# Seven block products in place of eight in one more quarter of two batches, and what moves with them

## The chip, the cores and the metric

The kernel runs on one core of a Trainium2 chip. The metric is the device time of one execution in microseconds (us), taken as the median of several runs. A profile shows one execution in detail; its times are counted from the first instruction.

## What is computed

Linear attention with cosine weights for 8 batches, 8 heads, 576 rows and 64 features, and behind it a channel mixer with a low-rank mixing over the sequence. Cut to what matters:

```python
r = np.maximum(x, 0.0)                                  # phi, of q and of k
phi = np.concatenate([r * c, r * s], axis=-1)           # cos and sin of the position
kv = np.einsum('bhsf,bhsd->bhfd', k_p, v)
x = num / den                                           # q_p @ kv over q_p @ sum(k_p)
h = xt @ U @ V                                          # rank 32, over the sequence
u = x + h.transpose(0, 2, 1)
out = u + np.maximum(u @ w_ch1, 0.0) @ w_ch2            # 512 -> 2048 -> 512
```

## The kernel before, in words

**Stages of a batch.** Each batch has 512 rows in the main part and 64 in a tail; the tails of two batches (a pair) are computed together. The attention of batch b gives x, then A (U against x), then u = x + VA. GpSimd, ScalarE and VectorE prepare q, k and v (`q_prep`, `k_prep` L305 and L307, `v_prep` L116). u in bfloat16 (`u_bf`, added by VectorE in `u_add`, L506) is transposed by DMAs that SP issues (`utr_dma`: L535 for the main part in two halves of features, L541 for the tail `uT_tl`). The first product (`hid = relu(u @ w_ch1)`) gives hid in 16 blocks j of 128 x 512. The second product reads hid and gives the output.

**Strassen in the first product.** A plain block (`g1_main`, L710) is 4 matmuls of 512 columns, and ScalarE's relu (L717). Four blocks (a quarter, m) can instead be taken as a 2 x 2 block product with 7 parts (`g1_part`, L653) of 4 matmuls of 256 columns: sums of weights `sa` (made once by VectorE, L591), differences of u^T `tb` (VectorE, `uT_form`, L608, four per batch), partial results that ScalarE copies out of PSUM (`pw`, L114), additions by VectorE (L678), and a relu of what was added. In batches 4 and 6 that relu is on ScalarE (L670), two slots later; elsewhere on VectorE (L675). One part is finished by ScalarE alone (L687). `HALF` (L1046) is the order of such a half of the first product: eight slots, in which the 7 parts take turns with 4 plain blocks. `MIXED` (L815) says which halves of which batch are done so: both in 3 and 5, the first alone in 4 and 6, and all 16 blocks of batch 7 by `LAST`. `FULL` is the list of batches with both.

**Strassen in the second product.** For batches 1 to 7 it is done in 7 parts of two halves (`W_SEQ`, L860: 1 1 2 6 6 2 7 5 5 7 3 3 4 4; `w_part`, L874, matmuls L892). Its left sides are S1 to S4, made of hid by VectorE (`hid_form`, L841, operations L857) in two halves of rows each. S3 is written over a block of hid; part 7 reads it, part 3 reads S4, part 6 S2, part 5 S1. The result is put together in `o_sb`: ScalarE copies parts 1, 6 and 5 out of PSUM (L114), VectorE adds parts 2, 7, 3 and 4 (L912), GpSimd adds u (`add_u`, L912 on POOL), and a DMA writes it out (L755, issued by GpSimd for batches below 6, else by SP).

**The order.** It is written out by hand: `slots` is a list of small units of TensorE work, `starts[b]` the number of batch b's first slot, here called G. A first product has 16 slots; an odd batch has 4 more for the tails of its pair (`g1_tail`, L741, which read `uT_tl`); a second product has 14. `put` hangs other work on a slot: it is issued behind that slot's matmuls. Each engine, SP's queue included, works strictly in the order in which its instructions were issued. `attention_plan` (L1129) hangs the attention of batch b on the slots of batches b - 2 and b - 1. For b = 5 and 7, G being the start of batch b - 1, the five `x_unit`s stand on slots G + 5, 8, 10, 12, 14 where batch b - 1 is in `MIXED`, and on G + 5, 8, 11, 13, 15 where it is in `FULL`; A, u and the transposes follow two slots and more after the last. `d0` (L1188) says which half of u is added and transposed first.

The two lines that decide where u's tail goes in these batches:

```python
late_t = 3 if b == 5 and b - 1 in FULL else 0 if b - 1 in FULL else 1 if b - 1 in MIXED else 0
put(*((u_at + 1, u_tail, *T1) if b < 4 else (u_at + 3 + d0 + late_t, u_tail, *X1S)))
put(u_at + 4 + d0 + late_t, utr_dma, 4, 5)
```

SP also carries the transposes of q (`qtr_dma`, L413 and L408) and the loads of q, k and v for the batch after (`loads`, L93, L80, L87). In the plan of batch 6 they stand on G + 23 and 24 (q's transposes) and G + 24 (the loads of q for batch 7), G being the start of batch 4.

Of the kernel before, what the change touches and what calls it, by code (L numbers as in the profile page):

```python
# [17 lines left out]
def kernel(  # L18
# [13 lines left out]
    B = 8  # L32
# [79 lines left out]
    def cast(eng, o, i):  # L112
        if eng is nc.scalar:
            nc.scalar.activation(out=o, in_=i, func=AF.Copy, bias=0.0, scale=1.0)  # L114
        else:
            eng.tensor_copy(out=o, in_=i)  # L116
# [150 lines left out]
    def bank(shape, dt, tag, bufs, name):  # L267
        if tag == "x":
            return ps.tile([P, 2, 512], FP32, tag="X", bufs=1, name=name)[:, 0, 0 : shape[1]]
        if tag in ("oA", "oB"):  # L270
            return ps_rest[1].tile(shape, dt, tag=tag, bufs=bufs, name=name)
        if tag == "O":
            t = ps_rest[2].tile([P, 2, 512], FP32, tag=tag, bufs=bufs, name=name)
            return t if len(shape) == 3 else t[:, 0, 0 : shape[1]]
        return ps.tile(shape, dt, tag=tag, bufs=bufs, name=name)
# [317 lines left out]
    def uT_block(b, dh, r):  # L593
        return uT[b][:, 2 * dh : 2 * dh + 2, 2 * r : 2 * r + 2, :].rearrange(
            "p d c t -> p d (c t)"
        )

    def uT_form(b, n):
        if b not in tb:
            tb[b] = pool.tile([P, 4, 2, 256], BF16, tag="tb", bufs=1, name="tb")  # L600
        t = tb[b]
        a, b_ = (
            (uT_block(b, 0, 1), uT_block(b, 0, 0)),
            (uT_block(b, 1, 1), t[:, 0]),
            (uT_block(b, 1, 1), uT_block(b, 0, 1)),
            (uT_block(b, 1, 0), t[:, 1]),
        )[n]
        V_.tensor_tensor(out=t[:, n], in0=a, in1=b_, op=ALU.subtract)  # L608
# [156 lines left out]
    def o_alloc(b, r):  # L765
        if (b, r) not in o_sb:
            o_sb[b, r] = pool.tile([P, 2, DM], FP32, tag="o_sb", bufs=2, name="o_sb")
        return o_sb[b, r]
# [43 lines left out]
                in_=o_s[i * TS : i * TS + TS, :],  # L812
            )

    MIXED = {3: (0, 2), 4: (0,), 5: (0, 2), 6: (0,)}  # L815
    FULL = [b for b, ms in MIXED.items() if 2 in ms]
    HD = DM // 2
    KB = NJ // 2
# [3 lines left out]
    def w2_block(i, h, r=slice(0, KB)):  # L822
        return w2_h[:, r, i, h * HD : h * HD + HD]
# [13 lines left out]
    def hid_block(b, i, r, rows=slice(0, KB)):  # L837
        h = hid[b].rearrange("p (k i) t -> p k i t", i=2)
        return h[:, rows, i, r * 256 : r * 256 + 256]

    def hid_form(b, n, half):  # L841
        if (b, n) not in s_forms:
            s_forms[b, n] = (
                hid_block(b, 0, 1) if n == 3 else
                pool.tile([P, KB, 256], BF16, tag=f"S{n}", bufs=1, name=f"S{n}")
            )
        r = slice(half * 4, half * 4 + 4)
        o = s_forms[b, n][:, r, :]
        if n == 1:
            a, b_, op = hid_block(b, 0, 1, r), hid_block(b, 1, 1, r), ALU.add  # L850
        elif n == 2:
            a, b_, op = s_forms[b, 1][:, r, :], hid_block(b, 0, 0, r), ALU.subtract
        elif n == 3:
            a, b_, op = hid_block(b, 0, 0, r), hid_block(b, 0, 1, r), ALU.subtract
        else:
            a, b_, op = hid_block(b, 1, 0, r), s_forms[b, 2][:, r, :], ALU.subtract
        V_.tensor_tensor(out=o, in0=a, in1=b_, op=op)  # L857
# [7 lines left out]
    def store_w(b, c, r):  # L865
        if b == 1:
            later.append(lambda: store(store_eng(b), b, c, o_sb[b, r]))
        else:
            store(store_eng(b), b, c, o_sb[b, r])
# [4 lines left out]
    def w_part(b, n):  # L874
        p, half = W_SEQ[n]
        lhs, rhs, to = {
            1: (lambda: hid_block(b, 0, 0), w2_block(0, 0), 0),
            2: (lambda: hid_block(b, 1, 0), w2_block(1, 0), 1),
            3: (lambda: s_forms[b, 4], w2_block(1, 1), 0),
            4: (lambda: hid_block(b, 1, 1), T[3], 2),  # L880
            5: (lambda: s_forms[b, 1], T[0], 0),
            6: (lambda: s_forms[b, 2], T[1], 0),
            7: (lambda: s_forms[b, 3], T[2], 2),
        }[p]
        lhs = lhs()
        opens = p in (1, 2, 7)
        if opens and half == 0:
            w_ps[to] = bank([P, DM], FP32, *(G3 if to else T1), f"w_ps{to}")
        res = w_ps[to].rearrange("p (g n) -> p g n", g=2)
        for k_ in range(half * 4, half * 4 + 4):  # L890
            for g in range(2):
                nc.tensor.matmul(  # L892
                    out=res[:, g, :], lhsT=lhs[:, k_, g * P : g * P + P], rhs=rhs[:, k_, :],
                    start=(opens and k_ == 0 and g == 0),
                    stop=(k_ == KB - 1 and g == 1), skip_group_check=not opens,
                )
        for f in ({0: (4,), 2: (3,)} if b == B - 1 else {0: (1, 2), 1: (4,), 2: (3,)}).get(n, ()):
            hid_form(b, f, 1)
        if half == 0:
            return  # L900

        def by_d(t):
            return t.rearrange("p c (d n) -> p d c n", n=P)

        def u(r, h):
            return u_bf[b][:, 2 * h : 2 * h + 2, 2 * r : 2 * r + 2, :]

        def o(r, h):
            return o_alloc(b, r)[:, :, h * HD : h * HD + HD]

        def add(eng, o_, x, y):
            eng.tensor_tensor(out=o_, in0=x, in1=y, op=ALU.add)  # L912

        def add_u(r, h):
            add(G_, by_d(o(r, h)), by_d(o(r, h)), u(r, h))

        if p == 1:
            cast(A_, o(0, 0), res)
            add_u(0, 0)
        elif p == 6:  # L920
            cast(A_, o(1, 0), res)
            add_u(1, 0)
        elif p == 5:
            cast(A_, o(1, 1), res)
        elif p == 2:
            add(V_, o(0, 0), o(0, 0), res)
        elif p == 7:
            add(V_, o(1, 1), o(1, 1), res)
            add_u(1, 1)
        elif p == 3:  # L930
            add(V_, by_d(o(0, 1)), u(0, 1), by_d(res))
            store_w(b, 0, 0)
        else:
            add(V_, o(1, 0), o(1, 0), res)
            store_w(b, 2, 1)
# [104 lines left out]
    slots, second, starts = [], [], {}  # L1040

    def lay(units, in_second):
        slots.extend(units)
        second.extend([in_second] * len(units))
# [3 lines left out]
    def first_units(b):  # L1048
        starts[b] = len(slots)

        def unit(names, m):
            def go():
                for n in names:
                    if n[0] == "s":
                        g1_main(b, 4 * m + int(n[1]))
                    else:
                        g1_part(b, m, int(n))

            return go

        for m in (0, 2):
            if m in MIXED.get(b, ()):
                lay([unit(n.split(), m) for n in HALF], False)
            else:
                lay([lambda j=j: g1_main(b, j) for j in range(4 * m, 4 * m + 8)], False)
        for i in range(4 * (0 < b)):
            n = 12 + 2 * i if b == 1 else (9, 11, 17, 18)[i] if b in MIXED else 8 + i
            beside.setdefault(starts[b] + n, []).append(
# [28 lines left out]
    def second_units(b):  # L1097
        lay([lambda n=n: w_part(b, n) for n in range(14)], True)
# [30 lines left out]
    def attention_plan(b):  # L1129
# [3 lines left out]
        def put(at, f, *a):  # L1133
            plan.append((at, lambda: f(b, *a)))
# [17 lines left out]
        else:  # L1152
# [19 lines left out]
            elif b - 1 in FULL:  # L1172
                kv_at, x_at = G + 1, [G + i for i in ODDX]
            elif b - 1 in MIXED:
                kv_at, x_at = G + 1, [G + i for i in X5]
# [17 lines left out]
        if odd:  # L1193
            late_t = 3 if b == 5 and b - 1 in FULL else 0 if b - 1 in FULL else 1 if b - 1 in MIXED else 0
            put(*((u_at + 1, u_tail, *T1) if b < 4 else (u_at + 3 + d0 + late_t, u_tail, *X1S)))
# [237 lines left out]
    def put(at, thunk):  # L1433
        todo.setdefault(at, []).append(thunk)

    put(15, lambda: gate(w2_bf[0:1, 4, 0:1]))
    s6 = starts[B - 2]
    for n in range(4):
        for m in (0, 2):
            put(starts[2] + (-4, -3, -1, 1)[n], lambda n=n, m=m: w1_form(n, m))  # L1440
            put(s6 - 6 + n, lambda n=n, m=m: w1_form(n, m + 1))
        for b in MIXED:
            put(starts[b] - 4 + n, lambda b=b, n=n: uT_form(b, n))
        put(s6 + 24 + n, lambda n=n: uT_form(B - 1, n))
        put(starts[B - 1] + len(LAST) + 5 + 2 * n, lambda n=n: tl_form(n))
    put(starts[3] - 2, split_o)
    put(70, release)
# [41 lines left out]
```

## Time and profile before

| | us |
|---|---|
| median of 3 runs | 291.23 (291.1 to 293.08) |
| the profiled execution | 291.12 |
| its span, first to last instruction | 289.3 |
| TensorE (PE) busy | 284.5 |
| VectorE (DVE) busy | 217.1 |
| ScalarE (ACT) busy | 173.3 |
| GpSimd (POOL) busy | 75.6 |
| first product of batch 4, first matmul | 160.13 |
| second product of batch 4 | 176.05 to 189.68 |
| first matmul of the tails of batches 4 and 5 | 204.7 |
| second product of batch 6 | 238.01 to 251.62 |

What lies between the span and the execution's own time is 1.8 us. Matmuls are pipelined: a row gives 379 ns for one of 512 columns, but the next starts after about 216 ns, so the spacing is read from long rows of the chain, not from the mean of one.

### The profile page before, as it was taken

To read this page: it belongs to the slowest core of one execution; us is meant where nothing else is said; L and a number is where in the kernel's file an instruction comes from. 1 tells how busy PE (TensorE), PEld (TensorE's weight loads), DVE (VectorE), ACT (ScalarE), POOL (GpSimd) and SP (SyncE) were. 2 spreads that over 40 slices of the span, in tenths; PEclk is the share of its full clock that TensorE was granted. 3 is DMA by queue.
4 is the path that set the end of the run, shared out by engine and by line. 5 is a ranking of instruction groups with operands and counts; after the bars stand their busy time and mean duration, and the time that the engine had idled before them with its cause. 6 is when DMAs were issued, how large, how long until landed. Compare 5 with 4: busy or idle time off the path is not lost.

```text
span 289.3 us, 7481 instructions
## 1 busy us (share of the span) xinstructions
PE 284.5 (98%) x3086; PEld 208.5 (72%) x3086; DVE 217.1 (75%) x440; ACT 173.3 (60%) x302; POOL 75.6 (26%) x111
## 2 busy tenths in 40 slices
PE   8999999999999999999999999999999999999995
PEld 6876455545987546876987656876888657999884
DVE  4879738886898777548896278848899579669954
ACT  2965651576587466986686577786795762167110
POOL 8330600050026301851043502341034003100320
PEclk9999999999999999999999999999999999999999
DMA  6999999999989999899929994589974301320023
GB/s 203 336 284 252 290 208 275 258 171 157 291 206 145 190 372 210 163 312 223 302 59 183 290 289 122 77 222 204 242 144 107 122 1 39 86 116 2 0 87 133
DMA packets 85447, 53.32 MB, mean 184 GB/s; under 512 B 53990, under 2 KB 83078, under 8 KB 85414
## 3 DMA queue, kind: packets, MB, share of 16 engines
q1 hardware_dynamic: 78998, 41.62, 63.1%
q0 software_dynamic: 6272, 11.17, 15.7%
q8 instruction: 24, 0.39, 0.6%
q14 instruction: 9, 0.07, 0.1%
q10 hardware_dynamic: 144, 0.07, 0.1%
HBM read 36.86 MB, written 9.44 MB: 160 GB/s over the span
## 4 chain that ended last, share of the span: by engine, by line
PE 98%; DVE 1%; issue 0%; DVEq 0%
PE w_ps L892 30%; PE g_ps L710 26%; PE al_ps L653 6%; PE gt_ps L741 5%; PE o_ps L781 5%; PE be_ps L653 5%; PE w_ps L202 3%; PE x_ps L439 3%; PE kv_ps L364 3%; PE ot_ps L801 2%; PE ot_ps L994 2%; PE a_ps L465 1%; PE va_ps L495 1%; PE t_ps L382 1%; PE t_ps L394 1%; PE g_ps L727 0%
## 5 line engine op out<-in xcount | busy, mean ns | idle before, releaser
L710 PE MATMUL g_ps<-uT,w_bf 128*128 128x512 bf16 x346 | 84.2, 379 | 0.0
L717 ACT ACTIVATE hid<-g_ps 128x512 bf16<-128x512 f32 x88 | 52.2, 597 | 35.8 <-PE g_ps L710 30.6
L912 POOL TENSOR_TENSOR o_sb<-o_sb,u_bf 128x512 f32<-128x512 f32 x21 | 29.8, 1419 | 123.8 <-ACT o_sb L114 106.2
L710 PEld LDWEIGHTS <-w_bf 128*128 128x128 bf16 x346 | 31.8, 98 | 29.1
L892 PEld LDWEIGHTS <-hid 128*128 128x128 bf16 x448 | 43.0, 98 | 6.3
L892 PEld LDWEIGHTS <-S 128*128 128x128 bf16 x336 | 32.5, 98 | 4.2
L678 DVE TENSOR_TENSOR hid<-pw,be_ps 128x512 bf16<-128x512 f32 x30 | 20.6, 686 | 19.4 <-ACT pw L114 11.1
L892 PE MATMUL w_ps<-w_bf,hid 128*128 128x256 bf16 x224 | 27.9, 273 | 0.0
L892 PE MATMUL w_ps<-T,hid 128*128 128x256 bf16 x224 | 27.9, 273 | 0.0
L114 ACT ACTIVATE pw<-al_ps 128x512 f32<-128x512 f32 x30 | 17.8, 596 | 15.6 <-PE al_ps L653 7.9
L892 PE MATMUL w_ps<-T,S 128*128 128x256 bf16 x224 | 26.9, 273 | 0.0
L114 ACT ACTIVATE o_sb<-w_ps 128x512 f32<-128x512 f32 x21 | 12.5, 597 | 19.7 <-PE w_ps L892 16.2
L912 DVE TENSOR_TENSOR o_sb<-o_sb,w_ps 128x512 f32<-128x512 f32 x21 | 14.3, 682 | 11.7 <-ACT o_sb L114 5.5
L506 DVE TENSOR_TENSOR u_bf<-x_bf,va_ps 128x1024 bf16<-128x1024 bf16 (+1 forms) x20 | 19.6, 998 | 3.4 <-PE va_ps L495 2.6
L449 DVE TENSOR_TENSOR x_bf<-x_ps,rec 128x512 bf16<-128x512 f32 x28 | 19.4, 692 | 1.0
L305 ACT ACTIVATE k_p<-kst,sinw 128x512 bf16<-128x512 f32 x26 | 17.8, 713 | 0.0
L116 POOL CAST v_ext<-vst 128x512 bf16<-128x512 f32 x24 | 15.8, 698 | 6.9 <-issue 3.2
L653 PEld LDWEIGHTS <-sa 128*128 128x128 bf16 x160 | 14.8, 98 | 3.3 <-issue 0.2
L741 PE MATMUL gt_ps<-uT_tl,w_bf 128*128 128x128 bf16 x256 | 16.4, 219 | 0.0
L781 PE MATMUL o_ps<-w_bf,hid 128*128 128x512 bf16 x64 | 15.6, 379 | 0.0
L755 POOL DMA_DIRECT2D out_dram<-o_sb x12 | 7.6, 631 | 30.3 <-DVE o_sb L789 22.8
L741 PEld LDWEIGHTS <-w_bf 128*128 128x128 bf16 x256 | 15.0, 98 | 0.4
(191 smaller groups left out, 495.0 us busy)
## 6 DMA issues: line engine op xcount, KB each, us to landing
qst<-in_q_dram SPq DMA_DIRECT2D x14, 512.0 KB, 5.9
kst<-in_k_dram SPq DMA_DIRECT2D x14, 512.0 KB, 7.8
vst<-in_v_dram SPq DMA_DIRECT2D x12, 512.0 KB, 8.3
out_dram<-o_sb POOLq DMA_DIRECT2D x12, 512.0 KB, 5.0
w_bf<-in_moe_w_ch_dram POOLq DMA_DIRECT2D x8, 512.0 KB, 10.3
out_dram<-o_sb SPq DMA_DIRECT2D x4, 512.0 KB, 3.7
qst<-in_q_dram SPq DMA_DIRECT2D x2, 640.0 KB, 5.8
kst<-in_k_dram SPq DMA_DIRECT2D x2, 640.0 KB, 13.8
```

What stands on the lines that cost most here:

```text
L114: nc.scalar.activation(out=o, in_=i, func=AF.Copy, bias=0.0, scale=1.0)
L305: nc.scalar.activation(out=o, in_=i, func=AF.Relu, bias=0.0, scale=w)
L449: nc.vector.tensor_tensor(out=x_of(b, c, rows).rearrange("p (g i d) -> p g i d", g=2, d=D), in0=view[:, :, :, 0:D], in1=rec[rows].unsqueez ...
L506: nc.vector.tensor_tensor(out=u_bf[b][:, d0 : d0 + n], in0=x_bf[b].rearrange("p c (d n) -> p d c n", n=P)[:, d0 : d0 + n], in1=t.rearrange ...
L653: nc.tensor.matmul(out=res[:, k_, :], lhsT=lhs[:, d, k_, :], rhs=rhs[:, d, :], start=(opens and k_ == 0 and d == 0), stop=(k_ == 1 and d = ...
L678: V_.tensor_tensor(out=o, in0=x, in1=res, op=ALU.add)
L710: nc.tensor.matmul(out=g_ps.rearrange("p (c t) -> p c t", c=4), lhsT=w1_bf[:, d, j * P : j * P + P], rhs=uT[b][:, d, :, :], start=(d == 0) ...
L717: nc.scalar.activation(out=hid[b][:, j, :], in_=g_ps, func=AF.Relu, bias=0.0, scale=1.0)
L741: nc.tensor.matmul(out=g_ps[:, jj, :], lhsT=w1_bf[:, d, j * P : j * P + P], rhs=uT_tl[pr][:, d, :], start=(d == 0), stop=(d == 3),)
L781: nc.tensor.matmul(out=o, lhsT=hid[0][:, j, cc * P : cc * P + P], rhs=w2_bf[:, j, :], start=(j == 0), stop=(j == NJ - 1),)
L892: nc.tensor.matmul(out=res[:, g, :], lhsT=lhs[:, k_, g * P : g * P + P], rhs=rhs[:, k_, :], start=(opens and k_ == 0 and g == 0), stop=(k_ ...
L912: eng.tensor_tensor(out=o_, in0=x, in1=y, op=ALU.add)
```

## The change

Four edits:

- `MIXED` has both halves for batches 4 and 6 too: 4 blocks in each go from plain to 7 parts. Since `FULL` is made of `MIXED`, batches 4 and 6 are in it now, and the plans of batches 5 and 7 take the other branch: x on G + 5, 8, 11, 13, 15; u and its transposes a slot later; the second half of u's features first (`d0` = 2); u's tail and its transpose on G + 26 and G + 27 for batch 5 (before: G + 21 and G + 22), and on G + 23 and G + 24 for batch 7.
- In the second product of batches 1 to 6 the second half of S3 is made one slot ahead of that of S4, where S4 was ahead.
- GpSimd's additions of u for parts 1 and 6 are issued behind VectorE's addition of part 2, both together.
- The differences of u^T come later: slots -3, -2, 0 and 2 from the batch's start (before: -4 to -1); for batch 7 slots -2, -1, 0 and 2 (before: -6 to -3).

```diff
-    MIXED = {3: (0, 2), 4: (0,), 5: (0, 2), 6: (0,)}
+    MIXED = {3: (0, 2), 4: (0, 2), 5: (0, 2), 6: (0, 2)}
...
-        for f in ({0: (4,), 2: (3,)} if b == B - 1 else {0: (1, 2), 1: (4,), 2: (3,)}).get(n, ()):
+        for f in ({0: (4,), 2: (3,)} if b == B - 1 else {0: (1, 2), 1: (3,), 2: (4,)}).get(n, ()):
             hid_form(b, f, 1)
...
         if p == 1:
             cast(A_, o(0, 0), res)
-            add_u(0, 0)
         elif p == 6:
             cast(A_, o(1, 0), res)
-            add_u(1, 0)
...
         elif p == 2:
             add(V_, o(0, 0), o(0, 0), res)
+            add_u(0, 0)
+            add_u(1, 0)
...
         for b in MIXED:
-            put(starts[b] - 4 + n, lambda b=b, n=n: uT_form(b, n))
-        put(s6 + 24 + n, lambda n=n: uT_form(B - 1, n))
+            put(starts[b] + (-3, -2, 0, 2)[n], lambda b=b, n=n: uT_form(b, n))
+        put(starts[B - 1] + (-2, -1, 0, 2)[n], lambda n=n: uT_form(B - 1, n))
```

## The prediction

> **What bounds the kernel now.** I read the page first (busy times and chain), then TensorE's waits and the chain in order of time, then the timelines of VectorE, SP and GpSimd around batch 4, where the change is.
>
> ```profile
> span 289.3 us, 7481 instructions
> PE 284.5 (98%) x3086; PEld 208.5 (72%) x3086; DVE 217.1 (75%) x440; ACT 173.3 (60%) x302; POOL 75.6 (26%) x111
> ...
> PE 98%; DVE 1%; issue 0%; DVEq 0%
> ```
>
> TensorE is busy for 98% of the span and makes 98% of the chain. A busy PE can still be stretched, so the list of TensorE's waits is needed; it has one line, at the start of the program:
>
> ```profile
> PE w_ps L202 <- DVE zero L125: 1.2, 1, 1.2
> ```
>
> In the chain in order of time (start, length, what) stalls shorter than a listed wait show as pieces that take longer than their like:
>
> ```profile
> 112.33 12.25 PE w_ps L892 x112
> ...
> 171.38 1.73 PE g_ps L710 x8
> ...
> 189.84 0.44 PE al_ps L653 x4
> ...
> 204.88 0.89 PE gt_ps L741 x16
> ...
> 222.14 0.54 PE al_ps L653 x4
> ```
>
> From these: a 512-column matmul costs 1.73 / 8 = 0.216 us of TensorE, a 256-column one 12.25 / 112 = 0.109. Four parts' matmuls take 0.44; at 222.14 they take 0.54, so batch 6 starts 0.1 late. From about 60 us on I find no other stall above 0.05. So removed TensorE work shortens the run one for one, and anything late for TensorE lengthens it.
>
> VectorE, the busiest helper, in batches 4 and 5; SP's queue; a GpSimd addition:
>
> ```profile
> 177.60 0.69 DVE L857 TENSOR_TENSOR S<-S,hid 128x1024 bf16<-128x1024 bf16 x1
> ...
> 181.34 1.28 DVE L857 TENSOR_TENSOR hid<-hid 128x1024 bf16<-128x1024 bf16 x2
> ...
> 212.23 1.54 DVE L857 TENSOR_TENSOR S<-hid,S 128x1024 bf16<-128x1024 bf16 x1
> ```
>
> ```profile
> 181.05 5.61 SPq L535 DMA_TRANSPOSE uT<-u_bf  x2
> 186.75 1.22 SPq L541 DMA_TRANSPOSE uT_tl<-u_tl  x1
> 188.07 1.21 SPq L413 DMA_TRANSPOSE q_tlT<-q_tl  x1
> 189.39 8.26 SPq L408 DMA_TRANSPOSE q_pT<-q_p  x2
> 197.70 0.62 SPq L93 DMA_DIRECT2D qst<-in_q_dram  x1
> 198.37 0.63 SPq L80 DMA_DIRECT2D qst<-in_q_dram  x1
> 199.04 1.34 SPq L87 DMA_DIRECT2D qst<-in_q_dram  x1
> ```
>
> ```profile
> 211.89 1.33 POOL L912 TENSOR_TENSOR o_sb<-o_sb,u_bf 128x512 f32<-128x512 f32 x1 [15.48 <-ACT o_sb L114]
> ```
>
> The S3 pair ends at 182.62, and part 7 of the second product, which reads it, starts at 182.68: no slack. SP needs 8.26 us for q's two transposes. And the S4 operation at 212.23 takes 1.54 us where its like takes 0.69, because it began while a GpSimd addition was running.
>
> **Part 1, the matmuls.** A quarter goes from 16 x 0.216 = 3.46 us to 28 x 0.109 = 3.06: 0.40 less, 0.79 in the two batches. Beside it, in each quarter: VectorE gets 3 additions of 0.69; ScalarE reads PSUM 8 times as before and gets 3 relus of 0.62. From 168 to 176 ScalarE was busy 5.2 us; 1.9 more fit. VectorE was busy 5.7; with 2.1 more it is full, so it has to be followed (part 2).
>
> The row against a rule: the Trainium skill, TensorE: Matmul & The Clock Gate, section Back-to-back issue gap, gives sustained spacings of 81 ns for 128 columns and 131 for 512, set by weight load and matmul together. A straight line gives an estimate of 98 for 256, and by it the quarter goes from 2.10 to 2.74 and the change costs 1.3 us. The trace disagrees: 216 and 109 in long rows. By the rows the change saves 0.79.
>
> **Part 2, x later, and S3 ahead of S4.** Batch 5's last x comes a slot later, behind VectorE's addition of part 4: PE is done with that part at about 175.4, the addition and the x (0.17, 0.20, 0.69) run to 177.4, where the trace has 176.51. A's matmuls read it at about 177.8: covered by 0.4. From the start of that last 0.69 at 176.7 the steps between starts, from the rows of 175 to 183, are 0.61, 0.72, 0.62, 0.39, 0.60, 0.60, 0.39, 0.60 (S1, S2, a q_prep, S3, S4, a q_prep, S4, S3) and the last takes 0.68: S3 is whole at 181.9. TensorE would now be at part 7 at 182.68 - 0.40 - 0.45 = 181.83, the 0.45 being u's tail matmuls and their gap (182.32 to 182.68 and 0.09), which come later now. A stall of 0.1; bounds 0 and 0.5. In batch 6 no q_prep stands between, so 0. ScalarE's relu of part 4, for which VectorE's second half of S4 waits, ends near 177.0, before S4 is due at 180.5. Were it late, S3 and both u_adds would queue behind it; the edit sets one S3 half free of that.
>
> **Part 3, GpSimd's additions.** Where they stood, VectorE no longer loses time: at 212.23 it gains 0.85, at 146.60 0.9. That ends no TensorE wait by itself: 0. Both additions now follow part 2's. In batch 5 that is at about 216.4. A k_prep that begins at 216.7 is held to about 218.1; the weight sums behind it run through while GpSimd waits (as at 219.84, where an addition took 2.61), then the second addition holds one of the next sums for about 0.6. VectorE's addition of part 3 ends near 222.15 (222.03 before), and batch 6's first matmuls wait for its bank: 0.1 more. Bounds: -0.1 (the old stall gone) and 1.4 (the second addition goes at once, and part 4 stalls 0.4 and batch 6 one more us). Part 4's addition and the stores, which wait for GpSimd, have over 1 us; at the end of the program the sums for the tails (L954) have 4 us.
>
> **Part 4, u and u^T.** The half of u^T that the first matmuls of batches 5 and 7 read is now the second transpose. Batch 5: VectorE's u_adds follow S3; the last starts at 183.4 and ends at 184.6; landing takes 3.0 to 3.7 us here, so 187.7 to 188.4, needed at 189.3: covered by 0.9. Batch 7 has about 2 us. Bounds: 0, and 2.9 by the slowest row (7.5 us at 110.53, behind loads of v). The later differences of u^T (0.42 each) are due two slots after the batch's start at the earliest; VectorE has a gap there: 0. Issue order on VectorE makes the addition of part 4 wait behind the first two; it has 1 us.
>
> **Part 5, u's tail.** Its transpose was issued at 186.75, landed 2.4 us later, and is read at 204.7: 15 us of cover. Now SP reaches it behind q's three transposes and three loads of q. SP: the second u^T at 184.65 takes 1.2 to 2.4 (181.05's pair shows both), so q_tlT goes at 186.0 to 187.2, by 0.9 to 2.1 earlier than 188.07, and so does the rest: the last load of q at 196.9 to 198.1 instead of 199.04. That load landed 7.0 us after its issue; now 203.9 to 205.1. A transpose issued directly behind a load landed 0.5 us after it (q_tlT at 120.67), so the tail of u^T lands at 204.4 to 205.6, middle 205.0. TensorE wants it at 204.7 less 0.3 (0.40 saved, 0.1 lost): 204.4. Stall 0.6. Bounds: 0, if it doesn't queue behind the loads (2.4 after its issue), and 3.2, if it lands 2.5 behind the load, as u^T at 110.53 did behind v. A stall here also hides part 3's 0.1. The loads of k behind it come 1.3 us of issue later, with over 8 us until they are read.
>
> **Sum.** -0.79 + 0.1 (S3) + 0.6 (tail) = -0.1 on the profiled execution's 291.12 (span 289.3 and 1.8 around it): 291.0. The median of the runs, 291.23, stands 0.1 above that execution; I leave that inside the range.
>
> **Rivals.**
> - *The tail is in time.* SP takes the short issue times and the queue empties sooner: -0.79 + 0.1 + 0.1 = 290.5. For it: 7 us of landing includes loads of k that were served in between. 25%.
> - *The tail is later still, and the kernel slower.* The DMA engines are full from 191 on; landing 2.5 behind the load gives a stall of 1.6 to 3.2. It decides from 0.7 us of stall (landing after 205.1) on; middle 292.2, up to 293.6. For it: the row at 110.53. Against: that one stood behind three loads of v that had themselves waited. 15%.
> - *GpSimd holds VectorE.* Two additions back to back keep the path that both use; part 3's upper bound, 291.12 - 0.7 + 1.4 = 291.8. The Trainium skill, SBUF — State Buffer, section Who interferes with whom, says that whoever issues first has it for the whole instruction. By that rule GpSimd's second addition could win. The 2.61 us at 219.84 show it losing. 5%.
> - *The half of u^T is late*: 7.5 us, twice: about 295. Against: no load is ahead of it. 3%.
> - *The 256-column matmuls don't keep their pace*, as at 222.14 (0.54 for four): 28 x 0.135 = 3.8, 0.3 more per quarter instead of 0.4 less: 291.8. The 1104 such matmuls of the trace speak against it. 1%. The rule of part 1 would lead to this side too.
>
> **How the numbers follow.** The forecast (a stall of 0.2 to 1.2 at the tails, 290.6 to 291.6) has 45%, the rivals as said, and 6% are left for a wait that I have not seen. The range 290.2 to 292.6 takes in the forecast, the tail in time, GpSimd and most of the later tail: 8 in 10. 1% of 291 is 2.9 us, about what a measurement of this kernel can tell from no change. Faster by that needs four times the saved work: 2%. Slower by it needs the late half of u^T or something unseen: 5%. Within 1%: 93%.
>
> **What would show it.** g_ps rows at L710 fall by 32 matmuls and L653 gains 56. In the chain: a piece of the tails (L741) near 204.4 with a gap ahead of it, or a wait of TensorE for the transpose of uT_tl, which SP issues near 198; if there is none, part 5 is wrong. A short gap before part 7 near 181.9 shows part 2; the 0.54 at batch 6's start shows part 3. A time outside 290.2 to 292.6 would mean a wait of TensorE that I have not named.

## The result, and the profile after

| | before | after |
|---|---|---|
| median of 20 runs each, us | 291.1 (290.73 to 293.08) | 294.18 (291.58 to 295.86) |
| ratio of the runs, 95% interval | | 1.008 [1.0055, 1.0104] |
| the profiled execution, us | 291.12 | 291.69 |
| its span, us | 289.3 | 289.9 |

The forecast was 291.0 (290.2 to 292.6) and no change within 1%. By the ratio of the runs the kernel became slower by 0.8%: clear of the noise, but inside that 1% (the two medians alone differ by 1.06%). Its median lies 1.6 us above the range. The profiled execution of after lies near the shortest of its own runs. Two more executions, profiled later beside a before of 291.61, took 296.31 and 296.83, more than any of the 20. In two of the 20 runs of after (295.05 and 295.86) the mean granted clock of TensorE is 0.994 and 0.993, in the others 0.998 or more. So there are two questions: what costs 0.6 in the profiled execution where 0.1 less was forecast, and what makes the runs of the same kernel differ by 4 us.

The page of after, against the lines shown for before. PE still has 98% of the span, but no longer 98% of the chain: VectorE (DVE) has 4% of it and a DMA 3%. The DMA is a load of v at the program's start (5.75 to 15.44 us), and almost half of VectorE's share lies at the start too. What bears on the change is the rest of VectorE's share, between 215.8 and 223.0.

```profile
span 289.9 us, 7553 instructions
PE 283.1 (98%) x3110; PEld 209.3 (72%) x3110; DVE 220.5 (76%) x446; ACT 175.5 (61%) x308; POOL 71.6 (25%) x111
...
PE 90%; DVE 4%; DMA 3%; SPq 0%; issue 0%; DVEq 0%
```

TensorE's waits in the same execution (total, times, longest). Before had only the one for `zero`. Of the new ones two lie in the first 45 us (0.4 and 0.2 us); the other two are both for VectorE's additions at L912:

```profile
PE al_ps L653 <- DVE o_sb L912: 1.0, 1, 1.0
...
PE w_ps L892 <- DVE o_sb L912: 0.3, 1, 0.3
```

They lie at the end of batch 5's second product. By the distances between matmuls TensorE loses 0.47 us ahead of part 4 (which starts at 220.14) and 1.16 ahead of batch 6's first matmul (at 223.04), where before lost 0.11. The timeline of VectorE there (start, length, what; x2 is a pair):

```profile
215.68 1.78 DVE L307 TENSOR_SCALAR k_p<-kst,cosw 128x512 bf16<-128x512 f32 x2
217.38 1.71 DVE L591 TENSOR_TENSOR sa<-w_bf 128x512 bf16<-128x512 bf16 x2
...
219.41 0.68 DVE L912 TENSOR_TENSOR o_sb<-o_sb,w_ps 128x512 f32<-128x512 f32 x1
220.00 1.71 DVE L591 TENSOR_TENSOR sa<-sa,w_bf 128x512 bf16<-128x512 bf16 x2
...
222.31 0.67 DVE L912 TENSOR_TENSOR o_sb<-u_bf,w_ps 128x512 f32<-128x512 bf16 x1
```

and of GpSimd:

```profile
215.84 2.62 POOL L912 TENSOR_TENSOR o_sb<-o_sb,u_bf 128x512 f32<-128x512 f32 x2 [20.00 <-DVE o_sb L912]
...
220.16 1.27 POOL L912 TENSOR_TENSOR o_sb<-o_sb,u_bf 128x512 f32<-128x512 f32 x1 [1.70 <-DVE o_sb L912]
```

The reader is to see three pairs of 1.7 to 1.8 us, each of which overlaps one of GpSimd's three additions, and that the additions of parts 7 (219.41) and 3 (222.31), for which TensorE waits, stand behind them. A pair of L591 that GpSimd leaves alone takes 0.74 (below).

SP's queue of after, around the transpose of u's tail:

```profile
187.32 6.33 SPq L408 DMA_TRANSPOSE q_pT<-q_p  x2
...
196.40 0.63 SPq L87 DMA_DIRECT2D qst<-in_q_dram  x1
197.13 2.00 SPq L541 DMA_TRANSPOSE uT_tl<-u_tl  x1
```

It is issued at 197.13 and lands 7.0 us later, at 204.09. TensorE starts the tail's matmuls at 204.15, right behind those before them: nothing is lost in this execution, and nothing is spare.

### The profile page after: what moved, and what is told of

It reads as the page before. It is cut to its first block, busy times and chain, and to the rows that moved or that the text cites. A ratio compares the mean times of both kernels' runs of the same rounds, so it can differ in the third digit from the quotient of the medians.

```text
span 289.9 us, 7553 instructions
## 1 busy us (share of the span) xinstructions
PE 283.1 (98%) x3110; PEld 209.3 (72%) x3110; DVE 220.5 (76%) x446; ACT 175.5 (61%) x308; POOL 71.6 (25%) x111
## 4 chain that ended last, share of the span: by engine, by line
PE 90%; DVE 4%; DMA 3%; SPq 0%; issue 0%; DVEq 0%
PE w_ps L892 28%; PE g_ps L710 24%; PE al_ps L653 7%; PE be_ps L653 5%; PE gt_ps L741 5%; PE o_ps L781 5%; DMA vst<-in_v_dram 3%; PE x_ps L439 3%; PE kv_ps L364 3%; PE ot_ps L801 2%; PE ot_ps L994 2%; DVE sa L591 1%; PE a_ps L465 1%; PE va_ps L495 1%; PE t_ps L382 1%; DVE k_p L307 1%
## 5 line engine op out<-in xcount | busy, mean ns | idle before, releaser
L710 PE MATMUL g_ps<-uT,w_bf 128*128 128x512 bf16 x314 | 77.0, 379 | 0.0
L717 ACT ACTIVATE hid<-g_ps 128x512 bf16<-128x512 f32 x80 | 47.4, 597 | 31.8 <-PE g_ps L710 26.6
L912 POOL TENSOR_TENSOR o_sb<-o_sb,u_bf 128x512 f32<-128x512 f32 x21 | 26.4, 1272 | 111.8 <-DVE o_sb L912 111.8
L710 PEld LDWEIGHTS <-w_bf 128*128 128x128 bf16 x314 | 29.1, 98 | 25.9
L678 DVE TENSOR_TENSOR hid<-pw,be_ps 128x512 bf16<-128x512 f32 x36 | 24.7, 686 | 18.3 <-PE be_ps L653 9.7
L114 ACT ACTIVATE pw<-al_ps 128x512 f32<-128x512 f32 x36 | 21.3, 595 | 18.1 <-PE al_ps L653 8.9
L912 DVE TENSOR_TENSOR o_sb<-o_sb,w_ps 128x512 f32<-128x512 f32 x21 | 14.3, 683 | 12.0 <-ACT o_sb L114 7.2
L653 PEld LDWEIGHTS <-sa 128*128 128x128 bf16 x192 | 17.7, 98 | 4.0 <-issue 0.2
L653 PEld LDWEIGHTS <-w_bf 128*128 128x128 bf16 x144 | 14.0, 98 | 4.7 <-issue 1.2
L741 PE MATMUL gt_ps<-uT_tl,w_bf 128*128 128x128 bf16 x256 | 16.4, 219 | 0.0
```

What stands on the lines that cost most here:

```text
L653: nc.tensor.matmul(out=res[:, k_, :], lhsT=lhs[:, d, k_, :], rhs=rhs[:, d, :], start=(opens and k_ == 0 and d == 0), stop=(k_ == 1 and d = ...
L678: V_.tensor_tensor(out=o, in0=x, in1=res, op=ALU.add)
L710: nc.tensor.matmul(out=g_ps.rearrange("p (c t) -> p c t", c=4), lhsT=w1_bf[:, d, j * P : j * P + P], rhs=uT[b][:, d, :, :], start=(d == 0) ...
L717: nc.scalar.activation(out=hid[b][:, j, :], in_=g_ps, func=AF.Relu, bias=0.0, scale=1.0)
L741: nc.tensor.matmul(out=g_ps[:, jj, :], lhsT=w1_bf[:, d, j * P : j * P + P], rhs=uT_tl[pr][:, d, :], start=(d == 0), stop=(d == 3),)
```

## The experiments

Two theories, and a rival. **T1**: GpSimd's two additions, back to back, hold VectorE at the end of batch 5's second product and cost 1.4 us in every run. **T2**: the tail's transpose, now behind q's transposes and loads on SP, lands late by an amount that differs from run to run; that is the spread and the higher median. **R**: something else, such as the new order of u^T's halves. Medians below are of 6 to 12 runs each, beside runs of before on the same chip.

**e1: the tail early.** 

```diff
-late_t = 3 if b == 5 and b - 1 in FULL else 0 ...
+late_t = 0 if b == 5 and b - 1 in FULL else 0 ...
```

> After with one number changed: the transpose of u's tail for batch 6 is issued on SP ahead of q's transposes and the loads of q, as far up as before. T2 (the tail's landing sets the median and the spread of after): the median comes down by about 2.5 us to 291.7, with the runs within about 1 us, and the profile keeps TensorE's waits of 0.47 and 1.05 us at the end of batch 5. T1 (the two additions on GpSimd are the whole of the loss): it stays at 294.2 with the spread of after. Rival R (the new order of u^T's halves or other transfers): 294.2 as well, with another wait at a batch's start in the slow runs.

Measured: 292.77 (292.5 to 294.77), before 291.32. The spread is gone (11 of 12 runs within 0.6 us), as T2 says, and the waits of 0.47 and 1.16 us stay. The median misses 291.7 by 1.1: u's tail, three slots earlier, makes TensorE wait about 0.9 us in batch 4 for VectorE's `u_bf` (ahead of L518). The late slot of the tail's matmuls has its reason; only the place of the transpose on SP has not.

**e2: the additions back.** `add_u(0, 0)` and `add_u(1, 0)` again behind the copies of parts 1 and 6, in all batches.

> After with GpSimd's two additions of u back behind parts 1 and 6, as before the change. T1: TensorE's waits of 0.47 and 1.05 us at parts 4 of batch 5 and 3 of batch 6 go (to under 0.2 us in sum), the profiled execution is about 1.4 us shorter than after's 291.69. If T2 alone makes the spread, the median is some 1.4 us under after's (292.8) and the spread stays as wide; if T1 makes the spread too, the median is 290.5 and the runs lie within 1 us.

Measured: 294.12 (291.82 to 297.67), before 291.32. Four of the 12 runs took 296.4 to 297.7, with a mean granted clock of 0.994 or less; the other eight have a median of 292.5. T1's two waits go, but as much comes elsewhere: 0.97 us ahead of part 7 of batch 4, and 0.24 and 0.5 in batch 6. The spread stays. Two of TensorE's waits in its profiled execution (294.46):

```profile
PE gt_ps L741 <- DMA uT_tl<-u_tl: 1.8, 1, 1.8
...
PE w_ps L892 <- DVE hid L857: 0.8, 1, 0.8
```

The first is T2 caught in the act; the second shows that the additions were moved for a reason. VectorE's S3 has no slack, and what stands ahead of it is held: beside GpSimd's addition at 178.89 a `q_prep` takes 1.38 us (at 179.13) where its like in after takes 0.47 (at 178.33), and all that VectorE has queued behind it, S3 too, comes 0.9 us later.

**e3: both undone.** e1's and e2's edits together.

> Both of these in one kernel: tail early and additions behind parts 1 and 6; what is left of the change is Strassen's algorithm in batches 4 and 6, S3 ahead of S4, and u^T's halves in the other order. T1 and T2 together: 290.3 to 290.6 in nearly all runs, about 0.6 us under the kernel before. Rival R: 292.5 to 294 with the spread kept.

Measured: 293.33 (292.59 to 295.05), before 291.32. That is 2.7 to 3.0 us over what T1 and T2 gave, and inside the time that the rival R gave. But its profile shows no wait for the tail's transpose. It collects the costs of both undoings (0.97 in batch 4 and 0.24 and 0.5 in batch 6 as in e2, 0.9 in batch 4 as in e1), and 0.4 twice around batch 5 that neither of them has. Undoing an edit everywhere is not the same as taking away its harm.

**e4: only the loads of q behind the tail.**

```diff
-at_load = (F + 8, ...
+at_load = (F + (12 if b == 6 else 8), ...
```

> After with the three loads of q for batch 7 issued four slots later, so that on SP the tail's transpose stands behind q's two transposes but ahead of those loads. If the loads are what holds the tail: its landing comes 3 us or more ahead of batch 6's need and the median is 291.7, as with the tail early. If q's transposes alone hold it: median and spread stay at 294.2. T1's waits of 0.47 and 1.05 us stay in both.

Measured: 292.17 (291.56 to 293.46), before 291.32. The tail lands at 200.3 where TensorE wants it at 204.6; the spread is half as wide and the median is 2.0 us under after's. T1's waits stay (0.48 and 1.16). Behind q's transposes alone the tail still takes 6.2 us from issue to landing (2.4 in before), but that leaves 4 us to spare. So it is the loads that take it past the time of its need.

**e9: both cures.** e4's edit, and the additions back at parts 1 and 6 in batch 5 alone.

```diff
         if p == 1:
             cast(A_, o(0, 0), res)
+            if b == 5:
+                add_u(0, 0)
...
         elif p == 2:
             add(V_, o(0, 0), o(0, 0), res)
-            add_u(0, 0)
-            add_u(1, 0)
+            if b != 5:
+                add_u(0, 0)
+                add_u(1, 0)
```

> The loads of q for batch 7 behind the tail's transpose (as in e4), and GpSimd's two additions of u behind parts 1 and 6 in batch 5 alone; in batches 4 and 6 they stay behind part 2. T1 (the two back to back additions cost 1.4 us in batch 5, and only there) with T2: the waits of 0.48 and 1.16 us at 220 and 222 us go, those of e2 at part 7 of batches 4 and 6 (0.97 and 0.24 us) don't come, and the median is 1.4 us under e4's 292.2: 290.8, narrow, some 0.5 us under the kernel before. Rival: the additions hold VectorE wherever they lie in batch 5 as well, and 292.2 stays.

Measured: 290.37 (290.04 to 291.05), before 291.25, ratio 0.9964 [0.9943, 0.9985]: 0.4% faster than before, clear of the noise though under 1%, and 3.8 us under after's median. Its span, TensorE's longest wait, and VectorE's rows at the same place:

```profile
span 288.4 us, 7553 instructions
...
PE w_ps L202 <- DVE zero L125: 1.2, 1, 1.2
```

```profile
217.56 0.75 DVE L591 TENSOR_TENSOR sa<-w_bf 128x512 bf16<-128x512 bf16 x2
...
219.22 0.74 DVE L591 TENSOR_TENSOR sa<-sa,w_bf 128x512 bf16<-128x512 bf16 x2
...
220.56 0.67 DVE L912 TENSOR_TENSOR o_sb<-u_bf,w_ps 128x512 f32<-128x512 bf16 x1
```

The pairs of L591 take 0.75 and 0.74 where after had 1.71, part 3's addition comes 1.75 us earlier, and TensorE has no stall at either place.

**e10: before, with the tail's transpose late.**

```diff
-put(u_at + 4 + d0 + late_t, utr_dma, 4, 5)
+put(u_at + 4 + d0 + late_t + 3 * (b == 5), utr_dma, 4, 5)
```

> The kernel before with one number changed: the transpose of u's tail for batch 6 is issued on SP three slots later, behind q's transposes and the loads of q for batch 7; no Strassen in batches 4 and 6, no additions moved. T2: the tail lands some 7 us after its issue, at 204 to 208 us, TensorE waits for it ahead of the tail's matmuls in most runs, the median goes up by 1.5 to 2.5 us to 293 or so, and the runs spread over 3 us or more. Rival R (it takes the new order of u^T's halves or the Strassen parts as well): 291.2, narrow.

Measured: 291.68 (290.94 to 296.0), before 291.25, ratio 1.0004 [0.9982, 1.0027]. The mechanism is there (in the profiled execution, 292.12, the tail lands at 205.7 and TensorE loses 1.28 us ahead of L741), the size is not: the median rises by 0.4, within the noise, not by 1.5 to 2.5, and one run of the 12 took 296.0. So the late place alone does not cost the 2 us; with the rest of the change it does. Why the loads ahead of it land earlier here than in the two later executions of after (last below) is open.

**e7: before, with the additions moved.** The edit of `add_u` alone, in all batches.

> The kernel before with GpSimd's two additions moved behind part 2 in all batches, nothing else. T1: TensorE waits 0.4 to 0.5 us at part 4 and 1.0 us at part 3 of batch 5 as in after, and the median is 292.6, narrow. Rival (the waits need part 2 of the change, the weights' sums at other places): under 0.3 us, 291.4.

Measured: 293.08 (292.74 to 294.82), before 291.25, ratio 1.006 [1.0038, 1.0082]. T1 holds by itself and is larger: TensorE loses 0.60 ahead of part 4 and 1.50 ahead of batch 6, against 0.11 before.

**e6: before, with Strassen's parts alone** (the edit of `MIXED`).

> The kernel before with Strassen's algorithm for the first half in batches 4 and 6 and nothing else (S4 ahead of S3, additions where they were); the order of u^T's halves and the late tail follow from it by the plan's own conditions. Forecast's own terms: 32 fewer matmuls are worth -0.79 us. T2 and e2's waits: +0.97 and +0.8 us at parts 7 and at the tail's products in batches 4 and 6, and the late tail: fastest runs at 292, median 294 or more, spread of 3 us. Rival (the edits beside Strassen's are what costs): 290.5 to 291, narrow.

Measured: 294.5 (294.07 to 295.22, 6 runs), before 291.25. The matmuls of TensorE cost 0.79 us less by the forecast (32 of 512 columns go, 56 of 256 come), and the kernel is 3.3 us slower. TensorE's losses: 0.96 ahead of part 7 and 0.84 at the end of batch 4, 1.05 at the end of batch 5, 0.24, 0.47 and 0.66 in batch 6, in sum 4.2; 291.12 - 0.79 - 0.1 (before's stall there) + 4.2 = 294.4, and the profiled execution took 294.29. The spread that I expected is absent: the tail lands at 204.5, but TensorE, late by then, wants it at 206.0.

**e11: e9, with the sums of u^T early.** The last edit of the change undone.

> The kernel with both cures (e9), with the sums of u^T at their earlier places, as before the change. The forecast priced their move at nothing: then 290.4. Rival (VectorE's order at a batch's end is full once Strassen's parts are there, as the waits of 0.84, 1.05 and 0.66 us at the ends of batches 4, 5 and 6 in e6 say): each early sum of 0.42 us ahead of the addition of part 3 makes TensorE wait about 0.4 us at the ends of batches 4, 5 and 6, so 291 to 292.5.

Measured: 293.53 (292.64 to 294.73, 6 runs), before 291.61, ratio 1.007 [1.0047, 1.0094]. That is 3.2 us over e9, 3.3 over e12 (next), which was measured beside it, and more than the rival's upper end. VectorE at the end of batch 4 (in brackets the idle time before, and what ended it):

```profile
190.54 0.42 DVE L608 TENSOR_TENSOR tb<-uT 128x512 bf16<-128x512 bf16 x1 [2.80 <-DMA uT<-u_bf]
190.88 0.68 DVE L522 TENSOR_TENSOR u_tl<-x_tl,va_ps 128x512 bf16<-128x512 bf16 x1
191.48 0.68 DVE L912 TENSOR_TENSOR o_sb<-u_bf,w_ps 128x512 f32<-128x512 bf16 x1
```

It isn't the 0.42 us of the sum. VectorE stands idle for 2.80 us because the sum, first in its order, waits for the half of u^T to land; part 3's addition is queued behind it, and TensorE loses 1.48 us. It loses 1.06 and 0.49 more at the ends of batches 5 and 6.

**e12: e9, with S4 ahead of S3 again.**

> The kernel with both cures (e9), with S4 ahead of S3 again. Part 7 of the second product reads S3, which then ends about 1 us later. With Strassen's shorter first product TensorE waits for it: 0.9 to 1.0 us in batch 4 and 0.2 to 0.8 us in batch 6, in sum 1.2 to 1.8, so 291.6 to 292.2. Rival (the waits of e2 and e6 at part 7 came from GpSimd's additions alone): 290.4.

Measured: 290.26 (290.06 to 291.17), before 291.61, ratio 0.9959 [0.9942, 0.9976], the same as e9. My expectation was wrong and the rival right: the waits at part 7 in e2 and e6 came from GpSimd's additions. TensorE's gap at part 7 of batch 4 is 0.05 us here and 0.06 in e9: in this kernel the order of S3 and S4 is worth nothing.

**Two more executions of after.**

> The changed kernel once more, for its profile. T2: when the time is near its median of 294.2, TensorE waits 2 us or more ahead of the tail's matmuls and the tail lands at 206 to 208; when it is near 291.7 the wait is under 0.2 us. Rival R: in a slow execution the extra time lies elsewhere.

> As the look before: time over 291.7 equals TensorE's wait ahead of the tail's matmuls (T2) within 0.3 us, or not (R).

Measured: 296.31 and 296.83, before 291.61. The extra time lies where T2 puts it. TensorE's longest wait in the first of them, and its chain in order of time:

```profile
PE gt_ps L741 <- DMA uT_tl<-u_tl: 2.5, 1, 2.5
```

```profile
199.17 8.36 DMA uT_tl<-u_tl
...
207.57 1.80 PE gt_ps L741 x16
209.37 0.44 PE x_ps L439 x8
209.81 2.47 PE gt_ps L741 x32
```

But it doesn't equal the wait: 4.6 us over 291.7 stand against a wait of 2.66, so T2 alone is not enough. The three pieces behind it take 4.71 us where e9's like take 0.89 + 0.26 + 1.79 = 2.94. The windows of that execution say why (TensorE's busy time and matmuls, granted clock, DMA share, GB/s):

```profile
196.00:204.00 8.00, 7.95 (x74) 1.00 1.20 181
207.30:211.60 4.30, 4.03 (x47) 0.60 0.85 241
207.72:211.12 3.40, 3.40 (x39) 0.50 0.92 279
212.00:216.00 4.00, 4.00 (x71) 1.00 0.28 38
```

The second row is a mean over a stretch that is wider than the drop. The third shows the drop itself: from 0.1 us after the wait the clock is granted at 0.50 for 3.4 us, and matmuls of 128 columns follow each other by 107 ns instead of 56. In the second execution it is 0.50 for 3.4 us as well, after a wait of 2.95. In the first this costs 1.8 us beside the wait of 2.66. The account of the first against 291.69: 2.66 (wait) + 1.77 (clock) + 0.75 (it comes to the tails later, as it does to all from 78 us on) - 0.47 (part 4's stall, hidden) = 4.7, measured 4.62.

Two things are not shown. No execution near after's median of 294.18 was profiled: that its loss is the same wait is inferred from e1 and e4, which take most of it away. And that the wait sets off the clock drop is argued from two executions: four of the 20 runs of after took 295.1 to 295.5 with a mean clock of 1.000, and two runs of before, 294.03 and 294.62, have 0.988 and 0.994 with no late tail in the program.

## Why the prediction was wrong

**Part 1, the matmuls: right.** It said -0.79. e9, in which nothing else waits, is 0.88 us below before by medians and 0.95 by profiled executions (290.17 against 291.12); 0.1 of that is the old stall at batch 6's start, which is gone too. The Trainium skill, TensorE: Matmul & The Clock Gate, section Back-to-back issue gap, has the sustained spacings by which an estimate came out 1.3 us slower. These runs disagree with them, as the rows of before did (216 ns for 512 columns).

**Part 2, S3: right in its cost** (0.06 of a forecast 0.1; S3 is whole at 181.60, where 181.9 was forecast), and by e12 it makes no difference which comes first.

**Part 3, GpSimd's additions: the first step that failed.** It took 0.1 and kept 1.4 as the bound; the stalls are 0.47 and 1.16 against 0.11 before, 1.5 in all. The sentence that failed is "the weight sums behind it run through while GpSimd waits". That was read from one row, where an addition took 2.61 us and lost. In after the two additions ran in 2.62 together, without giving way, and the third in 1.27 where e9's takes 2.28: which engine gives way differs from row to row, and in after VectorE lost all three. What decides it stays open. The rival "GpSimd holds VectorE" (291.8) is what the profiled execution of 291.69 shows. It had 5%.

**Part 4, u and u^T: 0 was right for the changed kernel**, but it hid what the later differences of u^T buy. Without them the kernel is 3.2 us slower (e11). Likewise the additions' move saves about 1.7 us in batches 4 and 6 (e2) while it costs 1.5 in batch 5.

**Part 5, u's tail: the second step that failed, in its size.** It put the stall at 0.6; the median lost about 2.2 by it, the first profiled execution nothing, the two later ones 2.66 and 2.95 with 1.8 for the clock behind each. Place, cause and the landing behind the loads were right. The tail landed 0.7 us behind the last load of q in the profiled execution (204.1 and 203.4) and 0.6 behind it in both later ones; 0.5 was forecast. What failed is "That load landed 7.0 us after its issue": in after's profiled execution it took 7.0 again, but 8.5 and 9.4 in the two later ones, and SP came to it at 198.4 and 198.0 instead of 196.4. A single row stood for something that varies by 2.4 us. And 0.6 of stall had no cover, so what varied upward went into the time in full. The rival "the tail is later still" had the mechanism, with 15% and 293.6 as its end; it lacked the clock drop, which adds 1.8 in the executions that show it.

**The sum.** Each against the before beside it, e9 is 0.9 us under, e4 0.85 over and after 3.1 over. So the matmuls and S3 give -0.9 (forecast -0.69), GpSimd's additions in batch 5 +1.7 (forecast nothing, as 0.1 was to be hidden) and the tail +2.2 (forecast 0.6). These differences add up to 3.1 whatever their causes; what the edits show is which of them takes each part off. The additions' part has a check of its own in the 1.5 us of stalls in the profile. e9 keeps the new order of u^T's halves and has nothing left to explain, so R is not needed. "No change within 1%" held by the ratio, but that was luck: the sum behind it was off by more than 3 us. The prediction said that a time outside its range would mean a wait that it had not named; it had named both waits and put their sizes too low. What is left open is what sets the landing of q's loads from run to run.

## What to carry to other kernels

A transfer that lands just in time is not priced by one profile: if the trace of one execution leaves it no slack, take the slowest landing of its like, and allow for what TensorE may lose in clock after a long wait. An edit that is tied to several others has two prices, what it costs in place and what its absence would cost; only undoing it in one batch at a time (e9) separated them. Where an engine in strict order issues a cheap operation that waits for a DMA, the price is what is queued behind it, not the operation.

## What the runs showed of the hardware

- The granted clock fell to 0.50 for 3.4 us after TensorE had waited 2.66 and 2.95 us (the two later executions of after), and stayed at 1.00 after 1.94 us (e2). The Trainium skill, TensorE: Matmul & The Clock Gate, section HAM oscillation — how this bites in real kernels, gives as the rule that TensorE should have no idle gaps of more than about 3.4 us, behind which it restarts at half speed. The half speed agrees with 107 ns against 56; but the drop followed shorter waits here, in both profiled executions that had one over 2 us. Two are too few for a threshold.
- The transpose of u's tail, issued behind loads of q on SP, landed 0.6 to 0.7 us behind the last of them in six executions (after three times, e2, e6 and e10), whatever that load took: 7.0 to 9.4 us from issue. A transpose of half of u^T landed 2.5 us behind a load of v (118.04 against 115.58, in before).
- GpSimd's addition lengthens a VectorE pair that it overlaps by 0.9 to 1.0 us (after), or is itself lengthened from 1.3 to 2.3 (e9) or 2.6 (before); the same two lines showed both outcomes in neighbouring kernels.
